# Twenty weight folds as ten units of 32x32-tile products, turned by VectorE

## The chip, the cores and the metric

The kernel runs on one NeuronCore of a Trainium2 chip. Its engines are named as the profile names them: PE is TensorE (PEld its weight loads), DVE is VectorE, ACT is ScalarE, POOL is GpSimd, and SP is SyncE, whose queue issues nearly all DMAs here. SBUF is the on-chip memory that all engines read; PSUM is the memory that TensorE writes and that VectorE and ScalarE read; this kernel keeps buffers (banks) of 128x512 numbers there, eight of them in the stage of the change. The metric is device time of one execution in microseconds (us), lower is better. Before the change three runs took 2378.09, 2379.88 and 2381.68 us; the median is 2379.88 us.

## What is computed

A sequence of 2048 rows of width 1024 is normalized; then a linear attention with 32 heads of width 32 runs beside a gated MLP, and their product is added to the input. In short:

```python
xn = layernorm(x)
q, k, v = heads(xn @ wqkv)                 # 32 heads of 32
pq, pk = q @ w_phi[h], k @ w_phi[h]        # one 32x32 matrix per head
phi = lambda p: concat(softmax(p), softmax(-p))
o = phi(pq) @ (phi(pk).T @ v) / (phi(pq) @ sum(phi(pk)))
s = o @ wo
g = silu((silu(xn @ w1) * (xn @ w3)) @ w2)
out = x + s * g
```

The step that the change touches is `pq = q @ w_phi[h]` and `pk = k @ w_phi[h]`. The kernel never forms q and k. It folds each head's 32x32 matrix into the 32 columns of that head in the weights, once, on the chip: `wk' = wk @ w_phi[h]`, `wq' = wq @ w_phi[h]`, for two weights of 1024x1024. After that, one product of xn with the folded weight gives pk or pq.

## The kernel before

All large products use fp32r operands that are split in a high and a low part, so that each product takes three passes. They are also done block by block in a scheme of seven products in place of eight (Strassen's kind); the seven are named by their left operands, in the order A11, A12, S2, S1, S3, S4, A22. Stages, by time in the profile: the gate and up products with w1 and w3 (to about 1130 us), the key, value and query heads (to about 1520), the down product with w2 (to about 2160), and the attention output with wo (to the end).

The change is in the first stage. It runs twice over 28 sections of the hidden width (`f`, once for each half of the rows, `tb`); a section is seven steps, one for each product, and `events` lists the steps in order. A step is 12 matmuls of 128x512 into a PSUM bank. A11, S2, S3 and A22 add up in a bank of kind b (two buffers), S1 and S4 in one of kind c (two buffers), and A12 alone uses bank a, which has one buffer. Partial sums are read while the section runs: ScalarE copies bank b after A11 (L625), VectorE adds bank a to that copy after A12 (L627) and adds bank b after S3 (L641), and so on. The next product into the same bank waits for that reader.

Beside the products, side work goes on, which each step carries in two lists, `before` (ahead of the step's matmuls) and `after` (behind them): loads of the next weights (`rw`), their sums and splits into operands `bo` (ScalarE casts the high part at L92, VectorE subtracts at L93), the preparation of the other half of the rows (`side_x`), of the key and value weights (`side_kv`, tiles `wkv`, `wkvo`), stores of the operands (`side_store`), and the folds. The order of all engines, SP's queue too, is written out by hand in this way; `room(step, cost)` moves a piece of VectorE work on to the first step in which VectorE's planned time stays under 2.55 us.

A fold (`fold`, L247) takes a piece of the transposed weight `wr` (128 columns of the weight on the partitions, four groups of 128 of them), and multiplies each of the four by a 128x128 block-diagonal matrix `bd` that holds four heads' `w_phi`. Only a quarter of `bd` is not zero. The product with `wr` as the stationary operand turns it as well, so that the result in PSUM (`pw`) has the weight's rows on the partitions; ScalarE copies it back to SBUF (L500) and SP stores it to DRAM. There are 32 folds. The first 12 run in the first 50 us, and `side_fold` spreads the other 20 over the steps from 67 on, one every 5 or 6 steps, each with its load 5 steps ahead and its store 2 steps behind. Four of the 20 belong to the key weight, and `side_kv` reads them back from DRAM; 16 are the query weight, which is read much later.

Of the kernel before, what the change touches and what calls it, by code (L numbers as in the profile page):

```python
# [8 lines left out]
F = mybir.dt.float32  # L9
# [8 lines left out]
P = 128  # L18
NT = S // P
ND = D // P  # L20
NF = FF // P
G = 8
# [7 lines left out]
def tile_kernel(ctx: ExitStack, tc: tile.TileContext, x, wkT, wqT, wv, wphi, wo, w1, w3, w2, out):  # L30
# [44 lines left out]
    wkv_d = [{n: dram.tile([P, 2, 4, 512], F, name=f"wkv_d{c}{n}") for n in BNAMES} for c in range(3)]  # L75
    wk_d = [[dram.tile([P, 512], F, name=f"wk_d{c}_{k}") for k in range(ND)] for c in range(2)]
    wq_d = [[dram.tile([P, 512], F, name=f"wq_d{c}_{k}") for k in range(ND)] for c in range(2)]

# [159 lines left out]
    def load_w(wT, dch, c, t=None):  # L238
        wr = blk("wr") if t is None else t
        nc.sync.dma_start(wr, wT[dch][:, 4 * c:4 * c + 4])  # L240
        return wr

    def fold(wr, c):

        pw = ps.tile([P, 4, P], F, name="pw", tag="tr", bufs=3)
        for g in range(4):
            nc.tensor.matmul(pw[:, g, :], wr[:, g], bd[:, 4 * c + g, :], start=True, stop=True)  # L247
        return pw

    folds = [(wkT, k, c, wk_d[c][k]) for c in range(2) for k in range(ND)]  # L250
    folds += [(wqT, k, c, wq_d[c][k]) for c in range(2) for k in range(ND)]

# [36 lines left out]

    phi_raw = flat(blk("phi")[:, :2]).rearrange("p (g f) -> p g f", f=DH)  # L290
    nc.sync.dma_start(phi_raw, wphi)
# [87 lines left out]
    def at(step, f, d=after):  # L379
        d.setdefault(step, []).append(f)  # L380
# [99 lines left out]
    def side_kv(c, k, s0):  # L480
# [8 lines left out]
        for n in BNAMES:  # L489
# [3 lines left out]
            at_ = store_quad(at_ + 1, wkv_d[1 + c][n][:, :, k], lambda src=src: (r + t2)[src], "wkvo", then)  # L493

    def side_fold(m, s0):
        wT, k, c, d = folds[m]
        w = []
        at(s0, lambda: w.append(load_w(wT, k, c)))
        at(s0 + 5, lambda: w.append(flat(fold(w[0], c))), before)
        at(s0 + 5, lambda: nc.scalar.copy(flat(w[0]), w[1]))  # L500
        at(s0 + 7, lambda: nc.sync.dma_start(d, flat(w[0])))

# [32 lines left out]
    for i in range(4, 8):  # L535
        side_x(i, FIRST_STEP + 13 * (i - 4))
    for m in range(FOLDS, len(folds)):
        side_fold(m, FIRST_STEP + 48 + 11 * (m - FOLDS) // 2)
    for m in range(8):
# [905 lines left out]
```

## Time and profile before

| what | value |
|---|---|
| median of three runs | 2379.88 us |
| the profiled execution, its own time | 2381.62 us |
| its span | 2379.8 us |
| TensorE busy | 2351.0 us (99%) |
| VectorE busy | 1760.9 us (74%) |
| ScalarE busy | 910.1 us (38%) |
| mean granted TensorE clock | 0.999 |

The page of the profile counts as busy time what an engine spends in instructions. The timeline merges neighbouring instructions of one line: start, busy time, engine, line, operation, tiles, shape and count. The start of a row minus the start of the row before it is what the earlier one took of TensorE's time, since its matmuls overlap at their ends. The view of the waits says who waited for whom. A matmul of type fp32 (as in the folds) is two matmul instructions in the trace, one of type fp32r is one.

### The profile page before, as it was taken

The page shows a single profiled execution, that of the slowest core. Times are in us where ns is not written, and L with a number is a line of the kernel's source. Part 1 is how long each engine was busy: PE and PEld are TensorE (multiplying, and loading weights), DVE is VectorE, ACT ScalarE, POOL GpSimd, SP SyncE. Part 2 cuts the span into 40 slices and gives each one's busy share as a digit, 9 for nine tenths or more (in the row PEclk, how much of TensorE's full clock was granted, in tenths as well). Part 3 has the DMA queues.
Part 4 walks back from the last instruction along what each step waited for, and adds up shares of the span by engine and source line. Part 5 has one row for each costly group of instructions (what it writes and reads, how often), then busy time and mean ns, then how long its engine had stood idle before and what let it go on. Part 6 is the DMA issues. An engine that isn't in the chain of part 4 may idle for free.

```text
span 2379.8 us, 37194 instructions
## 1 busy us (share of the span) xinstructions
PE 2351.0 (99%) x14348; PEld 1934.9 (81%) x14348; DVE 1760.9 (74%) x2729; ACT 910.1 (38%) x1597; POOL 257.6 (11%) x243
## 2 busy tenths in 40 slices
PE   7999999999999999999999999999999999999999
PEld 6788888888888888888788888887888888887887
DVE  8877788765688888875566666777678888786775
ACT  6445454543444554543212222334433333352000
POOL 1000000000000000000000000331012222213562
PEclk9999999999999999999999999999999999999999
DMA  5446699985998888865977878986435653478763
GB/s 215 146 155 212 230 354 332 328 266 186 289 303 283 292 306 289 268 209 195 384 287 277 306 253 307 364 315 249 159 124 151 204 177 133 156 245 272 213 179 103
DMA packets 291472, 578.00 MB, mean 243 GB/s; under 512 B 24912, under 2 KB 140768, under 8 KB 288608
## 3 DMA queue, kind: packets, MB, share of 16 engines
q1 hardware_dynamic: 284960, 552.56, 68.5%
q10 hardware_dynamic: 6336, 23.07, 2.5%
q8 instruction: 113, 1.85, 0.3%
q14 instruction: 63, 0.52, 0.1%
HBM read 372.64 MB, written 202.91 MB: 242 GB/s over the span
## 4 chain that ended last, share of the span: by engine, by line
PE 93%; DVE 3%; DMA 2%; ACT 1%; SPq 1%; issue 0%; POOL 0%; DVEq 0%; ACTq 0%; POOLq 0%
PE bankb L598 24%; PE bankb L1199 13%; PE bankc L598 12%; PE pm L1351 8%; PE bankb L794 7%; PE bankc L1199 6%; PE banka L598 6%; PE bankc L794 3%; PE banka L1199 3%; PE bankb L861 3%; PE banka L794 2%; PE bankc L861 1%; PE po L1336 1%; PE pkv L779 1%; PE pw L247 1%; PE banka L861 1%
## 5 line engine op out<-in xcount | busy, mean ns | idle before, releaser
L93 DVE TENSOR_TENSOR bo<-rw,bo 128x512 fp32r<-128x512 f32 x336 | 230.9, 689 | 158.2 <-ACT bo L92 155.4
L1199 PE MATMUL bankb<-bo,as 128*128 128x512 f32 x960 | 235.2, 389 | 1.2 <-ACT acc L1205 1.2
L1199 PEld LDWEIGHTS bankb<-bo,as 128*128 128x128 f32 x960 | 180.2, 188 | 39.0 <-ACT acc L1205 1.6
L92 ACT CAST bo<-rw 128x512 fp32r<-128x512 f32 x336 | 206.5, 617 | 13.8 <-DMA w_d2B<-w2o 3.4
L598 PE MATMUL bankb<-op0S,bo 128*128 128x512 f32 x672 | 164.6, 394 | 1.9 <-ACT op0S L92 1.2
L598 PE MATMUL bankc<-op0S,bo 128*128 128x512 f32 x672 | 162.2, 391 | 0.0
L1351 PE MATMUL pm<-wos,oT 128*128 128x512 f32 x672 | 161.1, 394 | 0.9 <-DVE oT L1342 0.9
L598 PE MATMUL bankb<-op1S,bo 128*128 128x512 f32 x672 | 161.4, 389 | 0.6 <-ACT u L633 0.6
L598 PE MATMUL bankc<-op1S,bo 128*128 128x512 f32 x672 | 161.2, 389 | 0.0
L598 PE MATMUL bankb<-op0A,bo 128*128 128x512 f32 x672 | 159.7, 391 | 0.8 <-DVE bo L93 0.5
L771 POOL MEMSET ev<- 128x32 f32 x32 | 4.1, 129 | 1427.1 <-DMA xoA<-xo_d0A 1073.2
L1199 PE MATMUL bankc<-bo,as 128*128 128x512 f32 x624 | 158.4, 389 | 0.0
L598 PE MATMUL bankb<-op1A,bo 128*128 128x512 f32 x672 | 157.6, 390 | 0.0
L598 PEld LDWEIGHTS bankb<-op0S,bo 128*128 128x128 f32 x672 | 126.3, 190 | 29.0 <-ACT op0S L92 1.6
L1351 PEld LDWEIGHTS pm<-wos,oT 128*128 128x128 f32 x672 | 124.7, 188 | 29.5 <-DVE oT L1342 1.7
L598 PEld LDWEIGHTS bankb<-op1A,bo 128*128 128x128 f32 x672 | 125.9, 188 | 27.4 <-DVE u L641 1.3
L598 PEld LDWEIGHTS bankb<-op1S,bo 128*128 128x128 f32 x672 | 126.1, 188 | 27.1 <-ACT u L633 1.0
L598 PEld LDWEIGHTS bankc<-op1S,bo 128*128 128x128 f32 x672 | 126.1, 188 | 26.2
L598 PEld LDWEIGHTS bankb<-op0A,bo 128*128 128x128 f32 x672 | 125.2, 188 | 26.9 <-DVE bo L93 0.8
L598 PEld LDWEIGHTS bankc<-op0S,bo 128*128 128x128 f32 x672 | 125.4, 188 | 25.6
L1199 PEld LDWEIGHTS bankc<-bo,as 128*128 128x128 f32 x624 | 117.2, 188 | 24.4
L1213 DVE TENSOR_TENSOR acc<-bankb,acc 128x512 f32<-128x512 f32 x152 | 102.0, 685 | 31.1 <-PE bankb L1199 31.1
(262 smaller groups left out, 4343.8 us busy)
## 6 DMA issues: line engine op xcount, KB each, us to landing
rw<-in_w SPq DMA_DIRECT2D x112, 512.0 KB, 4.4
hr<-h_d SPq DMA_DIRECT2D x56, 512.0 KB, 4.8
h_d<-h SPq DMA_DIRECT2D x111, 256.0 KB, 5.4
xoS<-xo_d0S SPq DMA_DIRECT2D x44, 512.0 KB, 6.2
xoS<-xo_d1S SPq DMA_DIRECT2D x44, 512.0 KB, 6.1
xoA<-xo_d0A SPq DMA_DIRECT2D x33, 512.0 KB, 4.9
xoA<-xo_d1A SPq DMA_DIRECT2D x33, 512.0 KB, 4.4
e_d<-eq ACTq DMA_DIRECT2D x32, 512.0 KB, 6.3
```

The lines of the kernel that those rows point to most:

```text
L92: nc.scalar.copy(hi, src)
L93: (by or nc.vector).tensor_sub(lo, src, hi.bitcast(F))
L247: nc.tensor.matmul(pw[:, g, :], wr[:, g], bd[:, 4 * c + g, :], start=True, stop=True)
L598: nc.tensor.matmul(bank[b], bos[tb, f][bn][:, w, k], ao[an][:, u, k], start=first and n == 0, stop=LAST[b] == an and n == 11, skip_group_c ...
L771: nc.gpsimd.memset(v[:, :, DH:], 1.0)
L779: nc.tensor.matmul(pkv[sl, m], e[:, m // 4, (m % 4) * P + 32 * h:(m % 4) * P + 32 * h + 32], v[:, 4 * (m % 4) + h], start=first and m == 0 ...
L794: nc.tensor.matmul(bank[b], xo[an][:, u, k], wb[bn][:, w, k], start=an in ("A11", "A12", "S1") and n == 0, stop=LAST[b] == an and n == 11, ...
L861: nc.tensor.matmul(bank[b], xo[an][:, u, k], wb[bn][:, w, k], start=an in ("A11", "A12", "S1") and n == 0, stop=LAST[b] == an and n == 11, ...
L1199: nc.tensor.matmul(bank[b], t[:, u, pos + k], bos[kb, bn, k][:, w], start=first and n == 0, stop=LAST[b] == an and n == 5, skip_group_chec ...
L1213: nc.vector.tensor_add(c, pb, c)
L1336: nc.tensor.matmul(po[32 * j:32 * j + 32, a, 64 * k:64 * k + 64], kvs[sl, j, c, k], et[sl, :, 4 * k + j], start=True, stop=True, skip_grou ...
L1351: nc.tensor.matmul(p, oTs[t, h][:, a, k], wos[c, 4 * h + k][:, b], start=n == 0, stop=n == 3 * ND - 1)
```

## The change

The 20 folds from step 67 on are replaced by ten units of another shape, at the steps 59, 68, 79, 89, 100, 110, 121, 131, 142 and 152. The first two units make the last four pieces of the key weight, the other eight the query weight.

- Operands. A unit now loads the transposed weight as it is into the room of `bd` (units 0 and 1: two pieces of 128x512, in runs of 128 numbers; units 2 to 9: one of 128x1024, a whole row of DRAM for each partition). `bd` is free by then, since only the first 12 folds need it. The matrices `w_phi` stay in `early_z`, which keeps them for the whole stage.
- Products. Instead of 128x128 by 128x128, a unit makes products of 32x32 by 32 x (32 nd): for each row strip j of the array (one of four heads) and each column strip q, `w_phi` of that head is stationary and a strided quarter of the weight moves. A unit has 16 products of 256 columns (units 2 to 9) or 32 of 128 columns (units 0 and 1). Each row strip writes a bank of its own: three of them are the banks of tag `tr`, which the transposes of x use too (named `pf`), and the fourth is bank a.
- Turning. The result is still transposed inside each 32x32 block. VectorE turns it with `transpose` from PSUM into the same room in SBUF: four instructions of 128x256 a unit, or eight of 128x128, in two pairs of places that `room` chooses at 0.7 us each. ScalarE's copies of `pw` are gone.
- DMA. A unit stores its result with one DMA in runs of 128 or 256 numbers. The next unit loads into the same room, so its load waits until that store has landed.

`room` now finds VectorE's time taken by the turns, and so it moves the pieces of `side_kv` some steps further on (its first piece ends at step 101 instead of 95, its last at 171 instead of 163).

```diff
@@ tile_kernel
-    wk_d = [[dram.tile([P, 512], F, name=f"wk_d{c}_{k}") for k in range(ND)] for c in range(2)]
-    wq_d = [[dram.tile([P, 512], F, name=f"wq_d{c}_{k}") for k in range(ND)] for c in range(2)]
+    wk_d = [[dram.tile([P, 512], F, name=f"wk_d{c}_{k}") for k in range(ND if c == 0 else 4)] for c in range(2)]
+    wk_late = dram.tile([4, P, 512], F, name="wk_late")
+    wk_d[1] += [wk_late[k] for k in range(4)]
+    wq_all = [dram.tile([ND, P, 512], F, name=f"wq_d{c}") for c in range(2)]
+    wq_d = [[wq_all[c][k] for k in range(ND)] for c in range(2)]
...
-    phi_raw = flat(blk("phi")[:, :2]).rearrange("p (g f) -> p g f", f=DH)
+    phi_raw = early_z.rearrange("p (g f) -> p g f", f=DH)
...
+    fold_free = [0]
+
     def side_fold(m, s0):
-        wT, k, c, d = folds[m]
-        w = []
-        at(s0, lambda: w.append(load_w(wT, k, c)))
-        at(s0 + 5, lambda: w.append(flat(fold(w[0], c))), before)
-        at(s0 + 5, lambda: nc.scalar.copy(flat(w[0]), w[1]))
-        at(s0 + 7, lambda: nc.sync.dma_start(d, flat(w[0])))
+        assert 1 < events[s0][2] < 6
+        w, banks = [flat(bd)], []
+        if m < 2:
+            gs_, nd = (4 + 2 * m, 5 + 2 * m), 4
+        else:
+            gs_, nd = (m - 2,), ND
...
+        def multiply():
+            banks.extend(ps.tile([P, 512], F, name="pf", tag="tr", bufs=3) for _ in range(3))
+            banks.append(ps.tile([P, 512], F, name="banka", bufs=BANKS["a"]))
+            for n, g in enumerate(gs_):
+                wn = w[0][:, 512 * n:512 * n + P * nd].rearrange("p (d k) -> p d k", d=nd)
+                for q in range(4):
+                    for j in (3, 0, 1, 2):
+                        sl = slice(32 * j, 32 * j + 32)
+                        nc.tensor.matmul(banks[j][32 * q:32 * q + 32, P * n:P * n + 32 * nd], phi_raw[sl, g], wn[sl, :, 32 * q:32 * q + 32],
+                                         start=True, stop=True, skip_group_check=True)
+
+        def turn(j):
+            for n in range(len(gs_)):
+                o = w[0].rearrange("p (d n f) -> p d n f", d=nd, f=DH)[:, :, 4 * n + j]
+                nc.vector.transpose(o, banks[j][:, P * n:P * n + 32 * nd].rearrange("p (d f) -> p d f", f=DH))
...
+        ready = max(s0 - 5, fold_free[0])
+        at(ready, load)
+        at(s0, multiply, before)
+        at_ = s0 - 1
+        for js in ((3, 0), (1, 2)):
+            at_ = room(at_ + 1, 0.7)
+            for j in js:
+                at(at_, lambda j=j: turn(j))
+        at(at_ + 2, store)
+        fold_free[0] = at_ + 4
...
-    for m in range(FOLDS, len(folds)):
-        side_fold(m, FIRST_STEP + 48 + 11 * (m - FOLDS) // 2)
+    for m, s0 in enumerate((59, 68, 79, 89, 100, 110, 121, 131, 142, 152)):
+        side_fold(m, s0)
```

The step of a unit decides between which two products it stands. Units 2, 4, 6 and 8 stand ahead of S2, straight behind A12; units 1, 3, 5, 7 and 9 stand ahead of S4; unit 0 stands ahead of S1. The rows that follow are from section 17 (the 18th), where unit 6 is. On TensorE, before: the two products, and the next fold one step on.

```order
L598 MATMUL bankb_3542<-op0A11_279,bo_3449 128x512 x12
L598 MATMUL banka_3565<-op0A12_280,bo_3477 128x512 [waits Activation_49]
L598 MATMUL banka_3565<-op0A12_280,bo_3477 128x512 x11
L598 MATMUL bankb_3542<-op0S2_281,bo_3500 128x512 [waits Activation_49]
L598 MATMUL bankb_3542<-op0S2_281,bo_3500 128x512 [waits DVE_49]
L598 MATMUL bankb_3542<-op0S2_281,bo_3500 128x512 x10
L247 MATMUL pw_3615<-bd_276,wr_3503 128x128 [waits DMAHW2_49,PE_49]
L247 MATMUL pw_3615<-bd_276,wr_3503 128x128 x3
```

Now unit 6 comes between A12 and S2, and its first small product goes into a new buffer of bank a, for which it waits for a DMA (the load of `bd`) and for DVE.

```order
L647 MATMUL bankb_3594<-op0A11_262,bo_3510 128x512 x12
L647 MATMUL banka_3617<-op0A12_263,bo_3533 128x512 [waits Activation_49]
L647 MATMUL banka_3617<-op0A12_263,bo_3533 128x512 x11
L524 MATMUL banka_3645<-bd_259,early_z_258 32x256 [waits DMAHW2_49,DVE_49]
L524 MATMUL pf_3642<-bd_259,early_z_258 32x256 [waits PE_49]
L524 MATMUL pf_3643<-bd_259,early_z_258 32x256 [waits PE_49]
L524 MATMUL pf_3644<-bd_259,early_z_258 32x256 [waits PE_49]
```

What moved: twelve more small products follow these four (the second to fourth column strip), and S2's matmuls behind them. Bank a's buffer before `banka_3645` is `banka_3617`, which VectorE reads when it adds A12's sum. On VectorE, before, the work around that sum (L627) was this.

```order
L93 TENSOR_TENSOR bo_3578<-rw_3252,bo_3578 128x512 [waits DMAHW0_49,Activation_49]
L128 TENSOR_TENSOR rw_3433<-rw_3433 128x512 [waits DMAHW6_49]
L129 TENSOR_TENSOR t2_3581<-rw_3433 128x512 [waits DMAHW5_49,DVE_49]
L93 TENSOR_TENSOR wkvo_3584<-wkv_3320,wkvo_3584 128x512 [waits PE_49,Activation_49]
L627 TENSOR_TENSOR h0_3563<-banka_3565,h0_3563 128x512 [waits DMAHW2_49,PE_49]
L93 TENSOR_TENSOR bo_3602<-rw_3252,bo_3602 128x512 [waits DMAHW1_49,Activation_49]
L93 TENSOR_TENSOR wkvo_3605<-wkv_3321,wkvo_3605 128x512 [waits Activation_49]
L93 TENSOR_TENSOR bo_3633<-rw_3433,bo_3633 128x512 [waits PE_49,Activation_49]
```

And this is VectorE's row of work at the same place now.

```order
L96 TENSOR_TENSOR bo_3630<-rw_3309,bo_3630 128x512 [waits DMAHW3_49,Activation_49]
L131 TENSOR_TENSOR rw_3494<-rw_3494 128x512 [waits DMAHW0_49]
L132 TENSOR_TENSOR t2_3633<-rw_3494 128x512 [waits DMAHW7_49,DVE_49]
L96 TENSOR_TENSOR wkvo_3636<-wkv_3357,wkvo_3636 128x512 [waits PE_49,Activation_49]
L676 TENSOR_TENSOR h0_3615<-banka_3617,h0_3615 128x512 [waits DMAHW4_49,PE_49]
L96 TENSOR_TENSOR bo_3674<-rw_3309,bo_3674 128x512 [waits Activation_49]
L530 STREAM_TRANSPOSE bd_259<-banka_3645 128x8x32 [waits DMAHW2_49,PE_49]
L530 STREAM_TRANSPOSE bd_259<-pf_3642 128x8x32
L96 TENSOR_TENSOR wkvo_3679<-wkv_3355,wkvo_3679 128x512 [waits DMAHW0_49,Activation_49]
L96 TENSOR_TENSOR bo_3702<-rw_3494,bo_3702 128x512 [waits Activation_49]
```

What moved: the four pieces of work ahead of the sum of bank a (L676 now, L627 before) are of the same kinds as they were; behind it stand the turns, which are new.

More of the change, by code (lines that the diff above doesn't have):

```diff
@@ L248, in fold @@
         return pw
-    folds = [(wkT, k, c, wk_d[c][k]) for c in range(2) for k in range(ND)]
-    folds += [(wqT, k, c, wq_d[c][k]) for c in range(2) for k in range(ND)]
+    folds = [(wkT, k, c, wk_d[c][k]) for c in range(2) for k in range(ND)][:FOLDS]
     def b_load(f):
@@ L1424 @@
         "wkT": lay(wqkv[:, D:2 * D]),
-        "wqT": lay(wqkv[:, :D]),
+        "wqT": wqkv[:, :D].T.reshape(G, P, D),
         "wv": wqkv[:, 2 * D:],
```

15 lines of the change are left out of this document (added).

## Prediction

> **What bounds the kernel now.** I read the page first (busy shares, then the chain that ended last), then the windows of the stage in which the 20 folds stand, then the timeline around one fold.
>
> ```profile
> span 2379.8 us, 37194 instructions
> PE 2351.0 (99%) x14348; PEld 1934.9 (81%) x14348; DVE 1760.9 (74%) x2729; ACT 910.1 (38%) x1597; POOL 257.6 (11%) x243
> PE 93%; DVE 3%; DMA 2%; ACT 1%; SPq 1%; issue 0%; POOL 0%; DVEq 0%; ACTq 0%; POOLq 0%
> 220.00:500.00 280.00, 280.00 (x1317) 234.33 (x1316) 218.97 (x347) 139.57 (x257) 0.00 (x0) 1.00 0.91 307
> ```
>
> The chain is TensorE's for 93%, and in the folds' stage (fourth line, columns: window, length, PE, PEld, DVE, ACT, POOL, clock, DMA share, GB/s) TensorE is busy 280 of 280 us at the full clock. There, what is taken from or given to TensorE's own row of work changes the time one for one; VectorE is idle for 61 us, ScalarE for 140.
>
> **What goes.** One fold on TensorE, and ScalarE's copies:
>
> ```profile
> 292.19 2.88 PE L598 MATMUL bankb<-op0S,bo 128*128 128x512 f32 x12
> 294.92 1.05 PE L247 MATMUL pw<-bd,wr 128*128 128x128 f32 x8
> 295.73 2.98 PE L598 MATMUL bankc<-op0S,bo 128*128 128x512 f32 x12
> 298.54 0.84 PE L598 MATMUL bankb<-op0A,bo 128*128 128x512 f32 x3
> L500 ACT COPY wr<-pw 128x512 f32<-128x512 f32 x18 | 10.6, 587 | 9.5 <-PE pw L247 9.5
> ```
>
> A product of twelve takes 294.92-292.19 = 2.73 us. The fold takes 295.73-294.92 = 0.81, and the product behind it 2.81, 0.08 more than its due: 0.90 us a fold. Twenty folds: -18.0 us, all on the path. The copies (20 of 0.59 us) were on ScalarE, which has room: 0.
>
> **What comes on TensorE.** No row shows 16 tiles of 32x32 at once. The nearest are the attention's products in 64x32 tiles (eight of them), and one fp32 product of 256 columns on the whole array:
>
> ```profile
> 2203.09 0.39 PE L1351 MATMUL pm<-wos,oT 128*128 128x512 f32 x1
> 2203.41 0.86 PE L1336 MATMUL po<-acc,kvs 64*32 64x64 f32 x64
> 2204.20 0.50 PE L1351 MATMUL pm<-wos,oT 128*128 128x512 f32 x1
> 2043.18 0.59 PE L1123 MATMUL us<-early_z,consts 128*128 128x256 f32 x2
> 2043.42 0.82 PE L1199 MATMUL bankb<-bo,as 128*128 128x512 f32 x2
> L1123 PE MATMUL us<-early_z,consts x2: 377/377/377, 2043.2 to 2043.4; 128*128 128x256 f32 x2
> ```
>
> The two instructions of the fp32 product of 256 columns start 0.59-0.377 = 0.21 us apart, so 64 columns stream in 0.053. The 64 instructions of the attention would need 3.4 us one after another and took 0.79: the eight tiles do run side by side (3.4/8 = 0.43) and the rest is the tail of the last one. A unit of 256 columns is 32 instructions on 16 tiles, two to a tile: 2x0.21 = 0.43 of streaming, some 0.2 until the last tile has started and 0.16 of tail, 0.79 by this estimate. Units 0 and 1 (64 instructions of 128 columns) stream for the same 0.43. As before and behind the attention's products some 0.2 us go to the change of shape (0.32 from the start of the last `pm` to the first `po` instead of 0.23, and a slower first product behind, as with the fold), I take 0.98 for each unit: +9.8 us. Lower end 0.59 a unit (the whole-array product, start to end); upper end 3.85 (second rival). If only eight tiles stream at a time, the row that is nearest, 0.43 more: +4.3 in all.
>
> [...]
>
> **The wait that comes with it.** Units 2, 4, 6 and 8 stand straight behind A12, and their first product writes bank a. So TensorE must wait until VectorE has added A12's sum, in four sections. In section 17:
>
> ```profile
> 384.68 2.88 PE L598 MATMUL banka<-op0A,bo 128*128 128x512 f32 x12
> 387.39 0.84 PE L598 MATMUL bankb<-op0S,bo 128*128 128x512 f32 x3
> 386.01 0.69 DVE L93 TENSOR_TENSOR bo<-rw,bo 128x512 fp32r<-128x512 f32 x1 [1.33 <-ACT bo L92]
> 386.62 0.69 DVE L128 TENSOR_TENSOR rw<-rw 128x512 f32<-128x512 f32 x1
> 387.34 0.69 DVE L129 TENSOR_TENSOR t<-rw 128x512 f32<-128x512 f32 x1
> 387.95 0.69 DVE L93 TENSOR_TENSOR wkvo<-wkv,wkvo 128x512 fp32r<-128x512 f32 x1
> 388.55 0.68 DVE L627 TENSOR_TENSOR h<-banka,h 128x512 f32<-128x512 f32 x1
> ```
>
> S2 starts at 387.39; the sum of bank a ends at 389.23, 1.84 later. Today nobody on TensorE waits for it. The new order has the same four kinds of work ahead of the sum in all four sections (a `wkvo` or `xo` split among them), and no fold between A11 and A12. From VectorE's end to TensorE's start another row tells the hop, in a wait of just this sort:
>
> ```profile
> 1149.92 2.23 PE L794 MATMUL bankc<-op2B,xoS 128*128 128x512 f32 x9
> 1153.03 0.76 PE L779 MATMUL pkv<-ev 128*32 128x34 f32 x64 [0.88 <-DVE ev L819]
> 1152.19 0.69 DVE L819 TENSOR_TENSOR ev<-bankc,ev 128x512 f32<-128x512 f32 x1 [1.96 <-PE bankc L794]
> 261.26 1.05 PE L247 MATMUL pw<-bd,wr 128*128 128x128 f32 x8
> 265.14 0.68 DVE L627 TENSOR_TENSOR h<-banka,h 128x512 f32<-128x512 f32 x1
> 264.89 2.88 PE L598 MATMUL bankb<-op0S,bo 128*128 128x512 f32 x12
> ```
>
> 1152.88 to 1153.03: 0.15. So a wait is 1.84+0.15-0.09 (the change of shape falls into it) = 1.9 us, four of them +7.6 us. All that TensorE has behind is held up with it; VectorE and ScalarE gain on TensorE by that. Lower end: in section 11 (last three lines) the sum ended only 0.93 behind S2's start, since a fold ahead of A12 had given VectorE time: 4x0.99 = 4.0.
>
> **VectorE's turns.** 32 of 128x256 and 16 of 128x128:
>
> ```profile
> L1179 DVE STREAM_TRANSPOSE acc<-acc 128x1024 f32<-128x1024 f32 x30 | 35.5, 1220 | 0.0
> L641 DVE TENSOR_TENSOR u<-bankb,u 128x512 f32<-128x512 f32 x14 | 9.6, 685 | 0.2 <-PE bankb L598 0.2
> ```
>
> 1220 ns for 1024 columns is at least 0.31 us for 256; an operation on 512 columns of PSUM takes 0.69. I take 0.37 and 0.22: 32x0.37+16x0.22 = 15.4 us, in the 61 idle ones. What may be late next is the sum after S3, for which A22 waits:
>
> ```profile
> 315.77 2.88 PE L598 MATMUL bankc<-op0S,bo 128*128 128x512 f32 x12
> 318.49 5.60 PE L598 MATMUL bankb<-op0A,bo 128*128 128x512 f32 x24
> 317.23 0.68 DVE L641 TENSOR_TENSOR u<-bankb,u 128x512 f32<-128x512 f32 x1
> ```
>
> Here it ended 0.58 us before A22 began, in a section that had a fold of 0.90 in between and eleven pieces of work on VectorE between the sums of bank a and b. Without the fold A22 would wait 0.90-0.58+0.15 = 0.47. In the new order eleven such pieces without a unit stand in sections 16, 19 and 22: 3x0.47 = +1.4 at most, +1.0 taken. The others have eight to ten, or a unit that gives VectorE time.
>
> **DMA.** Twenty loads and twenty stores become twelve and ten, of the same bytes, in runs of 512 B in the stores.
>
> ```profile
> rw<-in_w SPq DMA_DIRECT2D x16, 512.0 KB, 5.2
> xo_d0S<-op0S SPq DMA_DIRECT2D x15, 512.0 KB, 7.4
> SPq L256 <- DVE bo L93: 56.2, 14, 5.8
> ```
>
> The room is one, so a load waits on SP's queue for the store before it: 7.4 (a store in such runs) and 5.2 us, 12.6 from the last turn to the loaded room; the next unit comes at least 8 steps of 2.73 us behind the last turn, and 6 (16 us) behind the store's place in the queue. Queued behind the waiting load are the `rw` loads; those wait for VectorE 4 us each anyway (third line). I put it at 0, upper end 3 us.
>
> **Sum.** -18.0+9.8+7.6+1.0 = +0.4 us: 2381.62 (the profiled execution: 2379.8 of span and 1.8 around it) becomes 2382.0, and the median of runs, 1.74 lower, 2380.3. Within 0.2% (4.8 us), about what a measurement of this kernel can tell from no change.
>
> **Rivals.** First, faster: VectorE comes to bank a earlier (the 4.0 of section 11's row) and a unit costs 0.65, near the lower end: -18.0+6.5+4.0 = -7.5, 2372.4. For it: ScalarE, whose casts VectorE waits for, has 12 us less to do. Against: the 1.33 us in the row at 386.01 are ScalarE waiting for A11's bank, not for copies.
>
> Second, slower by the array: the two halves of an fp32 product follow each other in one tile, and if a product must wait in order behind them, a unit of 256 columns takes 16x0.21+0.4 = 3.85 us, one of 128 the same: +28.7 over my sum, 2409. [...] The attention's row speaks against it: 32 pairs at 0.053 would be 1.7 us, and it took 0.79.
>
> Third, slower by VectorE: with turns in its row, the sum after S3 comes late in all eleven sections that have no wait on bank a, by 0.47 and two turns' 0.3 us: 11x0.77-1.0 = +7.5, 2387.8. It decides from the point where eleven pieces or more stand between the two sums; for it the 0.58 above, against it the count of eight to ten in most sections.
>
> **How the numbers follow.** Forecast (within 0.2%) 0.50, with eight tiles at a time counted in (+4.3); first rival 0.19; second 0.06; third, with a load of the room that comes late, 0.25. So faster 0.19, same 0.50, slower 0.31. The forecast's own range is 2376 to 2385. For 8 in 10 it must reach down to most of the first rival (2373) and up past the third (2389); the second stays out.
>
> **What would show it.** Right: `pw` rows are left for 12 folds only; small products with an idle of about 1.7 us before them, put down to VectorE's sum of bank a, four times; about 1.0 us from the first small product to the next large one; turns of 0.3 to 0.4 us. Wrong: an idle before the small products put down to a DMA; waits of A22 for VectorE in most sections; or a unit of several us.

## The result, and the profile after

| | kernel before | changed kernel |
|---|---|---|
| median of 17 runs each | 2379.63 us (2378.09 to 2382.71) | 2385.06 us (2379.74 to 2390.81) |
| ratio, 95% interval | | 1.0021 (1.0014 to 1.0029) |
| profiled execution, its own time / span | 2381.62 / 2379.8 us | 2383.72 / 2381.9 us |
| TensorE busy | 2351.0 us | 2344.6 us |
| A12 of section 8 to A12 of section 26 (all units stand between) | 364.71 us | 366.75 us |

The change costs 5.4 us on the median, 0.2%. The forecast was 2380.3; the time lies in its range (2373 to 2389) and outside the forecast's own range by a hair (2376 to 2385). The runs of the changed kernel also lie wider apart, over 11 us instead of under 5; why is not shown.

The page's second line, and what TensorE waited for longest in the changed kernel (us in total, times, longest):

```profile
PE 2344.6 (98%) x14572; PEld 1920.8 (81%) x14572; DVE 1772.7 (74%) x2777; ACT 900.1 (38%) x1577; POOL 256.7 (11%) x243
PE pw L250 <- DMA room_b<-in_wkT: 7.4, 1, 7.4
PE banka L524 <- DVE h L676: 6.9, 4, 1.7
PE pt L221 <- DVE xt L216: 3.2, 1, 3.2
PE pm L1400 <- ACT acc L1102: 3.0, 1, 3.0
```

The first and third wait stand at the start and were there before (7.3 and 3.7). The second and fourth are new. The second is the forecast one: four waits of 1.7 us for VectorE's sum of bank a. The fourth, at the first product with `wo` some 1700 us later, stands nowhere in the prediction.

The stretch of the folds, answering the row shown of before (window, length, PE, PEld, DVE, ACT, POOL, clock, DMA share, GB/s), and two short windows in it:

```profile
220.00:500.00 280.00, 273.05 (x1484) 220.34 (x1483) 220.12 (x370) 126.33 (x231) 0.00 (x0) 0.99 0.87 287
328.90:332.30 3.40, 3.40 (x9) 2.67 (x8) 1.91 (x4) 0.44 (x1) 0.00 (x0) 0.50 1.08 392
451.80:455.20 3.40, 3.40 (x9) 2.66 (x10) 1.96 (x4) 0.81 (x2) 0.00 (x0) 0.50 1.14 314
```

TensorE is idle for 7 us of the 280, all of it the four waits, and for two stretches of 3.4 us its granted clock is 0.50 (half clock, in what follows). Each begins about a microsecond behind one of the waits. A profile is one execution, and half clock stands elsewhere too: in the profiled execution of before the clock is 0.50 from 62.1 to 65.5 us, in that of the changed kernel it is 1.00 there (first row before, second row changed):

```profile
62.10:65.50 3.40, 3.40 (x9) 2.62 (x10) 3.40 (x7) 1.10 (x3) 0.00 (x0) 0.50 0.32 133
62.10:65.50 3.40, 3.40 (x16) 2.81 (x15) 3.40 (x6) 1.53 (x3) 0.00 (x0) 1.00 0.17 70
```

The changed kernel comes to A12 of section 8 1.4 us earlier (199.01 instead of 200.40); a stretch of half clock costs 1.6 us, as shown below. So the two spans, 2.1 us apart, must not be set against the medians' 5.4 part for part. The first of the four waits (section 11), from the timelines of TensorE and VectorE:

```profile
261.84 0.69 DVE L96 TENSOR_TENSOR bo<-rw,bo 128x512 fp32r<-128x512 f32 x1 [1.33 <-ACT bo L95]
264.38 0.68 DVE L676 TENSOR_TENSOR h<-banka,h 128x512 f32<-128x512 f32 x1
265.12 0.40 PE L524 MATMUL banka<-bd,early_z 32*32 32x256 f32 x1 [1.74 <-DVE h L676]
265.46 0.39 PE L524 MATMUL pf<-bd,early_z 32*32 32x256 f32 x3
265.77 0.50 PE L647 MATMUL bankb<-op0S,bo 128*128 128x512 f32 x1
```

The sum ends at 265.06 and the first small product starts 0.06 later. From there to S2's first product it is 0.65 us; the last small ones start 0.34 after the first. A unit without a wait, and a unit of the other shape (64 instructions of 128 columns):

```profile
292.29 2.88 PE L647 MATMUL bankb<-op0S,bo 128*128 128x512 f32 x12
295.11 0.40 PE L524 MATMUL banka<-bd,early_z 32*32 32x256 f32 x1
295.75 3.01 PE L647 MATMUL bankc<-op0S,bo 128*128 128x512 f32 x12
298.60 1.75 PE L647 MATMUL bankb<-op0A,bo 128*128 128x512 f32 x7
204.54 0.29 PE L524 MATMUL banka<-bd,early_z 32*32 32x128 f32 x1
205.54 1.20 PE L647 MATMUL bankc<-op0S,bo 128*128 128x512 f32 x4
```

S3 is due to end at 292.29+2.72 = 295.01; the next product (S4) starts at 295.75 and takes 2.85 to its successor instead of 2.72: 0.87 us for the unit. The other shape takes 1.00 from its first small product to the next large one, and with what it loses ahead and behind 1.22: section 8 takes 21.59 instead of 20.37 before, where it has the same transpositions of x and no fold.

The half clock behind the wait in section 14, and the turns on VectorE (from the view of the tile `pf`: duration min/median/max in ns):

```profile
327.70 0.40 PE L524 MATMUL banka<-bd,early_z 32*32 32x256 f32 x1 [1.74 <-DVE h L676]
328.36 4.60 PE L647 MATMUL bankb<-op0S,bo 128*128 128x512 f32 x12
332.79 2.88 PE L647 MATMUL bankc<-op0S,bo 128*128 128x512 f32 x12
L530 DVE STREAM_TRANSPOSE bd<-pf x36: 272/406/444, 208.7 to 486.7; 128x256 f32<-128x256 f32 x24, 128x128 f32<-128x128 f32 x12
```

S2 takes 332.79-328.36 = 4.43 us; behind a unit at full clock a product takes 2.85. Whole sections say the same: section 14 takes 23.31 us here and 21.75 in a kernel below that has the same wait and no half clock, so one such stretch costs 1.6 us. And the wait at the first product with `wo`, of before and then of the changed kernel (timeline of TensorE):

```profile
2164.82 1.71 PE L1336 MATMUL po<-acc,kvs 64*32 64x64 f32 x128
2166.47 5.22 PE L1351 MATMUL pm<-wos,oT 128*128 128x512 f32 x21
```

```profile
2165.34 1.71 PE L1385 MATMUL po<-acc,kvs 64*32 64x64 f32 x128
2170.03 4.96 PE L1400 MATMUL pm<-wos,oT 128*128 128x512 f32 x21 [2.98 <-ACT acc L1102]
```

Nothing in this part of the program was changed.

### The profile page after: what moved, and what is told of

Read it like the earlier page. It is cut to its first block, busy times and chain, and to the rows that moved or that the text cites. A ratio compares the mean times of both kernels' runs of the same rounds, so it can differ in the third digit from the quotient of the medians.

```text
span 2381.9 us, 37605 instructions
## 1 busy us (share of the span) xinstructions
PE 2344.6 (98%) x14572; PEld 1920.8 (81%) x14572; DVE 1772.7 (74%) x2777; ACT 900.1 (38%) x1577; POOL 256.7 (11%) x243
## 4 chain that ended last, share of the span: by engine, by line
PE 91%; DVE 3%; DMA 3%; ACT 1%; SPq 1%; issue 1%; POOL 0%; DVEq 0%; ACTq 0%; POOLq 0%
PE bankb L647 24%; PE bankb L1248 13%; PE bankc L647 12%; PE pm L1400 8%; PE bankb L843 7%; PE bankc L1248 6%; PE banka L647 5%; PE bankc L843 3%; PE banka L1248 3%; PE bankb L910 3%; PE banka L843 2%; PE bankc L910 1%; PE po L1385 1%; PE pkv L828 1%; PE banka L910 1%; DMA op2T<-wkv_d1T 1%
```

## The experiments

Each kernel is compared with the kernel before, run beside it on the same chip. The stretch from A12 of section 8 to A12 of section 26, which holds all ten units or, in before, all 20 folds, serves as a second measure of time; its length is free of what the rest of the program does. Half clock and waits are those of the one profiled execution of each kernel. "Code shifted by 64" means that 64 instructions whose results nobody uses stand ahead of TensorE's work; why follows below.

| kernel | median us | ratio to before (95%) | section 8 to 26, us | waits for bank a | half clock in it | wait at first `wo` product, us |
|---|---|---|---|---|---|---|
| before | 2379.63 | | 364.71 | 0 | 0 | 0 |
| changed | 2385.06 | 1.0021 (1.0014 to 1.0029) | 366.75 | 4 | 2 | 3.0 |
| units 2, 4, 6, 8 one step later | 2381.29 | 1.0006 (0.9997 to 1.0015) | 362.79 | 0 | 1 (6.8 us) | 2.8 |
| before, four folds into bank a | 2387.99 | 1.0030 (1.0019 to 1.0041) | 372.19 | 4 | 0 | 0 |
| changed, no turns | 2385.04 | 1.0020 (1.0011 to 1.0029) | 363.63 | 4 | 0 | 3.4 |
| six units behind A12 | 2398.25 | 1.0075 (1.0061 to 1.0089) | 369.21 | 6 | 1 | 3.2 |
| no unit behind A12 | 2392.06 | 1.0047 (1.0035 to 1.0060) | 355.96 | 0 | 0 | 4.1 |
| the same, code shifted by 64 | 2388.69 | 1.0031 (1.0018 to 1.0043) | 355.96 | 0 | 0 | 0 |
| before, code shifted by 192 | 2385.03 | 1.0020 (1.0011 to 1.0029) | 364.71 | 0 | 0 | 3.1 |
| before, code shifted by 64 | 2381.56 | 1.0007 (0.9998 to 1.0016) | 364.71 | 0 | 0 | 0 |
| changed, code shifted by 64 | 2378.98 | 0.9993 (0.9984 to 1.0002) | 366.76 | 4 | 2 | 0 |
| the same, waits filled by 16 products | 2385.58 | 1.0021 (1.0011 to 1.0030) | 370.62 | 0 | 0 | 0 |
| the same, filled by 8 | 2381.99 | 1.0007 (0.9997 to 1.0016) | 363.57 | 0 | 0 | 0 (2.4 elsewhere) |
| changed, one unit behind A12, code shifted by 64 | 2374.00 | 0.9972 (0.9960 to 0.9983) | 358.45 | 1 | 0 | 0 |

The theory at first was the prediction's: four waits for bank a, to which the trace had added half clock behind them. Its rivals were that the waits only take up time another wait would take, and that VectorE's turns are what costs.

### Four units one step later

```
-    for m, s0 in enumerate((59, 68, 79, 89, 100, 110, 121, 131, 142, 152)):
+    for m, s0 in enumerate((59, 68, 80, 89, 101, 110, 122, 131, 143, 152)):
```

> Units 2, 4, 6 and 8 stand one step later (80, 101, 122, 143), ahead of S1 instead of S2, so that VectorE has read bank a long before. Theory of the wait (the four waits for VectorE's sum of bank a, 1.9 us each in the trace of the change, and the stretches of 3.4 us at half the clock that follow two of them, 1.6 us each, are the loss; units themselves cost some 9 us for the 18 that the folds took): 7 to 10 us faster than before, about 2371, no wait of TensorE in the stage, granted clock as in the kernel before, and runs as close together as those of before. Theory of VectorE (its 48 turns and the side work that they push on are the loss, and a wait of TensorE only shows it): the wait turns up at another product, and the time stays 0 to 6 us above before. Theory of the transfers (stores in short runs, one room, and the 3.0 us wait at the first wo product): 0 to 5 us above before.

```profile
PE pt L221 <- DVE bd L530: 3.4, 1, 3.4
PE pm L1400 <- ACT acc L1102: 2.8, 1, 2.8
```

All four waits are gone, but unit 2, now at step 80, holds the three transposition banks when the transpositions of x at the next steps want them: one wait of 3.4 us, with 6.8 us of half clock at it. In the stretch there is a gain (4.0 us shorter than in the changed kernel), and the wait at the first `wo` product stays. The 7 to 10 us under before that were expected on the median did not come: 1.0006 is no difference that can be told from none.

### The waits alone

In the kernel before, the folds at steps 79, 100, 121 and 142 write bank a instead of a transposition bank (three of them are moved to that place by 1 or 2 steps):

```
+        if in_a:
+            pw = ps.tile([P, 512], F, name="banka", bufs=BANKS["a"]).rearrange("p (g n) -> p g n", g=4)
```

> The kernel before, with its 20 large folds; only four of them are put into bank a straight behind A12, at steps 79, 100, 121 and 142, as units 2, 4, 6 and 8 are in the change. Theory of the wait: four waits of about 2.0 us, +8 us, and up to four stretches at half the clock of up to 1.7 us each: 8 to 13 us slower than before, with a wider spread of runs. Theories of VectorE and of the transfers: none of their causes is here, so within 1 us of before.

```profile
PE banka L250 <- DVE h L631: 6.3, 4, 1.7
```

7.4 us more than before, a little under the 8 to 13 expected; in the stretch 372.19-364.71 = 7.5. The four waits alone cost 1.9 us each, with no unit and no turn in the program, and none is followed by half clock. The wait at the `wo` product is not there.

### No turns

```
-            for j in js:
-                at(at_, lambda j=j: turn(j))
```

> The change without VectorE's 48 turns (left out; the folded weights of the last ten units are then not what the reference has, and all the rest runs on them; the places of all other work are unchanged). Theory of the wait: within 2 us of the change, the four waits still there at 1.7 us of idle. Theory of VectorE: 4 us or more faster than the change, at or below the kernel before. Theory of the transfers: as the change.

```profile
PE banka L524 <- DVE h L674: 6.9, 4, 1.7
PE pm L1398 <- ACT acc L1100: 3.4, 1, 3.4
```

The time is that of the changed kernel, and both new waits are as they were: the 48 turns cost nothing. The stretch is 3.1 us shorter than in the changed kernel, and all of it lies in the two sections that had half clock there (14 and 20: 21.75 and 21.77 here, 23.31 and 23.34 there); the other sections agree to 0.06 us. So the difference is the clock's and not the turns'.

### Six units behind A12

```
+    for m, s0 in enumerate((58, 72, 81, 93, 102, 114, 123, 135, 144, 156)):
```

> The change with its ten units at the steps 58, 72, 81, 93, 102, 114, 123, 135, 144 and 156: six of them straight behind A12 instead of four. Theory of the wait: six waits of 1.9 us, that is 3.8 us more than the change, and 0 to 3 us more at half the clock: 8 to 13 us slower than before. Theories of VectorE and of the transfers: the same work, so as the change, 3 to 7 us slower than before.

```profile
PE banka L524 <- DVE h L676: 9.8, 6, 1.7
PE bankb L647 <- ACT u L682: 8.5, 2, 8.1
```

Six waits, as planned; with them 13 us more than the changed kernel. But the 8.1 us are a new wait near 578 us that has nothing to do with bank a (it comes back in the next kernel), so of this run only the stretch counts: 369.21, of it 1.6 for one half clock, so 367.6 against 363.6 with four waits and none. Section by section, against the kernel below that has no unit behind A12, the six waits cost 1.6 to 1.9 us each, 10.7 together; 0.9 more goes to section 11, where a unit at step 81 stands near transpositions of x (one wait of 0.7).

### No unit behind A12

```
+    for m, s0 in enumerate((59, 67, 87, 96, 108, 116, 124, 136, 144, 152)):
```

> The ten units stand behind the products of S2, S1 or S3 at steps 59, 67, 87, 96, 108, 116, 124, 136, 144 and 152, none behind A12 and none beside a transposition of x. Theory (each wait of TensorE for VectorE's sum of bank a costs its 1.74 us, and two of the four are followed by 3.4 us at half clock that cost 1.7 us more): no wait for bank a by the products of the units, no stretch of half clock between 200 and 500 us, and the first stage some 10 us shorter than in the changed kernel; the 3 us wait of TensorE ahead of the first product with wo stays, so about 2374 us, 0.25% under the kernel before. Rival (the units themselves cost about what the folds did): within 2 us of the changed kernel's 2385.

In the stretch the theory holds: 355.96, which is 363.63-355.96 = 7.67 us under the kernel with four waits and no half clock, and 8.75 under the kernel before. Of the 7.67, 0.28 is a wait of A22 in section 19; the sections with the four waits are 1.83 to 1.86 us longer each, 7.4 together. But the time is 12 us over before. Two lines of TensorE's waits, two of SP's between 515 and 592 us, and one of ScalarE's timeline:

```profile
PE bankb L647 <- ACT u L682: 13.3, 1, 13.3
PE pm L1400 <- issue: 4.1, 1, 4.1
```

```profile
SPq L167 <- DVE wkvo L96: 24.3, 1, 24.3
SPq L167 <- PE bankb L647: 12.4, 1, 12.4
575.72 0.63 ACT L680 ACTIVATE h<-h 128x512 f32<-128x512 f32 x1 [16.37 <-DVE h L676]
```

With other steps for the units, `room` puts the last pieces of `side_kv` later, and the loads of the next half's `op1A` on SP's queue wait 24.3 us for VectorE's splits in them. The stores of `h` stand behind those loads in the queue, so the tiles that VectorE and ScalarE need come free late, and TensorE waits 13.3 us for ScalarE. Half clock stands at that wait too (566.2 to 583.3 us), and section 26 takes 35.34 us instead of 19.04, 16.3 more. The six-waits kernel has the same wait at the same place. This chain is read from the order of the queue and the waits; no run takes it apart, so it is argued and not shown.

### Where TensorE's code is cut

The wait ahead of the first product with `wo` remained. The profile names ScalarE for it in the changed kernel, "issue" (nothing that the profile shows) in the kernel with no unit behind A12, and a DMA in one run below; it is there in all kernels with the ten units and not in the two that have folds. Two theories: the change has 18 DMAs fewer, which moves the order of the semaphores that DMAs share; or it is TensorE's own code. The queue "q8 instruction" of before and of the changed kernel (packets, MB):

```profile
q8 instruction: 113, 1.85, 0.3%
q8 instruction: 115, 1.88, 0.3%
```

1.85 MB in 113 packets are 16.4 KB each. TensorE has 14,348 products, as many weight loads and 330 waits and the like in before, 29,026 instructions in all, and 29,026/113 = 257 to a packet; in the changed kernel 29,473/115 = 256. In both traces packet n of this queue (from 0) starts when TensorE has begun between 256n+150 and 256n+449 of its instructions, for every n. So these packets are read here as TensorE's code, 256 instructions each. Counted in the trace in order of start, from 0, the first product with `wo` is instruction 23,553 in before, 1 behind a multiple of 256, and 24,000 in the changed kernel, 192 behind one (the units have 224 products and 224 weight loads more than the folds, 448 = 256+192, and there is one wait fewer). In the changed kernel TensorE stops just before number 24,001. A packet of the queue starts in that pause, at 2167.78, and has landed at 2168.66; TensorE goes on 1.4 us after that. In all seven kernels that stop like this the last packet landed 1.3 to 1.6 us before TensorE went on. The instructions ahead are the attention's 128 products and 128 weight loads, 256 instructions in 1.71 us.

To shift the code, n small products of the identity matrix, which nobody reads, go ahead of TensorE's first work, in its idle time (each is four instructions; with the waits that come with them the count at the first `wo` product moves by 66 for 16 of them and by 193 for 48):

```
+    pad = [ps.tile([P, 512], F, name="pad", tag="tr", bufs=3) for _ in range(3)]
+    for m in range(16):      # 48 in the kernel shifted by 192
+        nc.tensor.matmul(pad[m % 3][:32, :32], ident[:32, :32], ident[:32, :32], start=True, stop=True)
```

The kernel with no unit behind A12, shifted by 64:

> The kernel with the units behind S2, S1 and S3, and ahead of TensorE's first work 16 small products of 32x32 (64 instructions of TensorE) whose results nobody reads. The trace loads TensorE's code in blocks of 256 instructions, and in the changed kernel the first product with wo stands at the border of two blocks, right behind 256 instructions that take 1.7 us. Theory (TensorE waits there for its code): the border lies elsewhere, the 3 us wait ahead of the first product with wo is gone, and the time is 1.3 to 3 us under that of the same kernel without the 16 products, about 2371 us. Rival (the wait is for a transfer of wo, whose place in the order of transfers has moved): the wait of 3 us stays, and the time is the same.

The kernel before, shifted by 192, which puts its first `wo` product where the changed kernel has it:

> The kernel before with 48 small products of 32x32 (192 instructions of TensorE) ahead of TensorE's first work, in its idle time, whose results nobody reads: the border of two code blocks then lies at the first product with wo, as in the changed kernel, and nothing else of the change is made. Theory (code): TensorE waits some 3 us ahead of the first product with wo, and the time is 1.3 to 3 us over the kernel before, about 2382 us, less what an earlier start at full clock may give, up to 1.7 us. Rival (order of transfers): no wait there, and the kernel before's time.

The changed kernel, shifted by 64 (448+64 = 512, so its code is cut, to one instruction, where that of before is):

> The changed kernel with the 16 small products ahead of TensorE's first work. Theory (code): the four waits for bank a stay as they are, 6.9 us in all, the 3 us wait ahead of the first product with wo is gone, and the time is 1.3 to 3 us under the changed kernel's, about 2383 us. Rival (order of transfers): wait and time as in the changed kernel, 2385 us.

TensorE's timeline, of the kernel before shifted by 192 and of the changed kernel shifted by 64:

```profile
2162.38 1.71 PE L1339 MATMUL po<-acc,kvs 64*32 64x64 f32 x128
2167.15 2.19 PE L1354 MATMUL pm<-wos,oT 128*128 128x512 f32 x5 [3.06 <-DMA wos<-wo_d]
```

```profile
2164.86 1.71 PE L1388 MATMUL po<-acc,kvs 64*32 64x64 f32 x128
2166.50 5.26 PE L1403 MATMUL pm<-wos,oT 128*128 128x512 f32 x21
```

The wait comes into a kernel that has nothing of the change, and goes out of the changed one with all of its 22 DMAs in their order. The theory of the code holds, the one of the order of the DMAs falls. In time: +5.0 us on the kernel before (1.0020), -6.1 on the changed kernel's median (2378.98 against 2385.06, run at different times, each against before on its own chip: 0.9993 against 1.0021), -3.4 on the kernel without units behind A12 (of 5 and 6 runs, with intervals that overlap, so this figure alone would not show it). The first two are more than the 3 us of the wait, and more than the 1.3 to 3 expected. In the trace of the shifted kernel before, 3.4 us of half clock follow the wait (2167.5 to 2170.9), worth some 1.6 by the sections above; half clock is there too in five of the other six kernels with such a wait, and in the changed kernel's one profiled execution it is not. 3.1+1.6 = 4.7 is near the 5.0, but that profiled execution took 2382.56, 2.5 under its kernel's median, so the likeness proves little: the wait is shown, and what the medians lose beyond it is in part open.

A counter-test, the kernel before with 16 of the small products:

> The kernel before with 16 small products (64 instructions) ahead of TensorE's first work instead of 48: the same kind of added work, but the border of the code blocks lies some 128 instructions behind the first product with wo. Theory (the place of the border alone decides): no wait ahead of the first product with wo, and the kernel before's time within 2 us. Rival (the added products themselves cost time, or any shift does): slower by a third of the 5.0 us that 48 products cost, or more.

1.0007 (0.9998 to 1.0016), no wait: neither the small products themselves nor a shift as such is what costs.

### The waits filled, and where half clock follows

In the changed kernel shifted by 64, TensorE multiplies identity matrices into one of the unit's own banks while it would wait for bank a:

```
+            if m in (2, 4, 6, 8):
+                for _ in range(16):      # 8 in the second kernel
+                    nc.tensor.matmul(banks[0][:, :P], ident, ident, start=True, stop=True, skip_group_check=True)
```

> The changed kernel with the 16 small products ahead of TensorE's first work, and ahead of the products of units 2, 4, 6 and 8 sixteen products of the 128x128 identity with itself, into one of the unit's own banks, which the unit's products then overwrite: TensorE works through the 1.74 us in which it waited for bank a, and the border of the code blocks stays where it is. Theory (a wait of 1.74 us beside a unit's small products is what takes the clock to half): no stretch of half clock between 200 and 500 us, and 1.7 us less for each stretch that there was, two in the profiled execution without the filling: about 2376 us against 2379. Rival (the clock falls by the unit's small products, or at random): stretches of half clock stay, and the time is 2379 to 2381.

> As the kernel with the filled waits, but with eight identity products ahead of each of the four units instead of sixteen, which took 3.7 us there, twice the wait of 1.74 us: eight take some 1.85 us, so TensorE works through the wait and hardly longer (0.1 us for each unit). The border of the code blocks moves by 128 instructions and lies some 60 instructions behind the first product with wo, in work that takes longer than the load. Theory (the wait beside the small products takes the clock to half): no stretch of half clock between 200 and 500 us, section lengths as with the waits but without the sections of 23.3 us, and 1 to 3 us less than the 2379.0 of the same kernel without filling. Rival (half clock comes by the small products, or costs nothing on the median): 2379 to 2380.

Sixteen took 3.7 us, not the 1.87 that they were meant to take (each is two matmul instructions), so the stretch is 7.0 us longer than with four bare waits (4x1.8), and the kernel says only that no half clock came in it. With eight the work fits the wait (1.9 us), and the stretch is 363.57, as long as with four bare waits and no half clock (363.63), 3.2 under the kernel it is made from, which had two half clocks. Eight filled waits in these two kernels, none followed by half clock; the bare ones, of units or of folds, were followed by it in 5 of 23 in the six profiled executions that have them. By these counts alone, eight in a row without it would come by chance once in seven.

The times in the traces say more. In their clock records each stretch of half clock that ends within the span is 3.413 us long or a whole multiple of it, and in each execution the stretches begin whole multiples of 3.413 us apart (in before at 14.31 and 62.10 us: 14 multiples; in the changed kernel at 14.85, 328.88 and 451.76 us: 92 and 36). Counted on from these starts, an execution divides into intervals of 3.413 us, and every wait has a place in one. The changed kernel's four began 0.50, 0.89, 1.32 and 2.77 us into an interval, and half clock followed the first two of these. Of all 19 bare waits ahead of units:

| the wait began, us behind the start of an interval | waits | half clock in the next interval |
|---|---|---|
| 0.07 to 0.91 | 5 | 5 |
| 0.98 to 3.07 | 14 | 0 |

A wait of about 1.15 us near 60 us, which all 14 kernels have (with one of 0.6 close behind it), shows the same: the five that began 0.15 to 0.75 us into an interval were followed by half clock, as in before (0.75), and the other nine, as in the changed kernel (3.17), were not. Units without a wait never were (72, of which 16 began in the first 0.91 us). So at these places half clock goes with the wait, when it falls early in an interval. Three limits stay. Only two of the eight filled waits began that early (0.67 and 0.76), so the filling itself is tested by two cases. Of the four waits ahead of folds one began at 0.45 and was not followed. And near 1158 us TensorE waits for `xoA` 1.09 us in before and 1.31 in the changed kernel, both from 0.51 us into an interval, and the clock stays at 1.00. Why is open.

The median did not follow: 2381.99, above the 2378.98 of the unfilled kernel, where 2376 to 2378 were expected. Its trace has two waits that the other has not, 1.9 us at 605 us for VectorE's operand `bo`, and this:

```profile
2177.58 0.81 PE L1391 MATMUL po<-acc,kvs 64*32 64x64 f32 x58
2180.79 0.31 PE L1391 MATMUL po<-acc,kvs 64*32 64x64 f32 x6 [2.40 <-issue]
```

The fillers move the code by another 128. At the first `wo` product that is harmless, but another border now falls into a later group of the attention's products, between the 58th and the 59th of 64 that wait for nobody; the instruction that comes late is number 24,513 = 24,001+512. By this reading the code is late at yet another place, and 3.4 us at half clock follow (2182.4 to 2185.8).

### One unit behind A12

```
+    for m, s0 in enumerate((59, 68, 79, 89, 101, 110, 122, 131, 143, 152)):
```

and the 16 small products ahead of TensorE's first work.

> The changed kernel with the 16 small products ahead of TensorE's first work, and units 4, 6 and 8 one step later, behind the products of S2 instead of A12; unit 2 keeps its place. Theory (waits for bank a): one wait of 1.7 us is left of four, and with three waits go 3 times 1.74 us and, as far as half clock followed them, 1.7 us each for up to two: 5 to 8.6 us under the 2379.0 of the same kernel with four waits, so 2370 to 2374 us, 0.3% or more under the kernel before. Rival (the waits only move time that another wait then takes): 2377 to 2379 us.

```profile
PE banka L527 <- DVE h L679: 1.7, 1, 1.7
220.00:500.00 280.00, 278.25 (x1521) 224.80 (x1520) 227.54 (x382) 129.16 (x238) 0.00 (x0) 1.00 0.90 296
```

2374.0 us, 0.9972 (0.9960 to 0.9983): under both kernels, at the upper end of the 2370 to 2374 expected. The stretch is 358.45, 2.5 over the kernel with no wait (1.8 for the wait, 0.7 for two waits of A22 of 0.3), and 8.3 under the changed kernel. The rival that the waits only take up time which another wait would take falls.

## Why the prediction was right or wrong

The time was inside the range, and the sum for the part that was summed was near: +0.4 forecast, -1.1 measured in the stretch without half clock. But +5.4 came in all, since a term was missing. That the range held is luck: its upper part stood for VectorE's turns coming late and for a late load of the room, and neither came.

- **Folds removed: -18.0.** Right. From A12 to A12 a section with one fold takes 19.95 us, one without 19.04: 0.91 each, 18.2.
- **Ten units at 0.98: +9.8.** Near, slightly over-sized. Eight of 0.87 and two of 1.22: +9.4. The case that the sum is built on (sixteen tiles at once) holds, and the eight-tiles case and the second rival fall: 32 instructions take 0.65 us in all. (That rival's 16x0.21+0.4 is 3.76, not 3.85, so its +28.7 would be +27.8.) The change of shape costs 0.13 behind a unit and 0.1 ahead of it. The sign "about 1.0 us from the first small product to the next large one" came for two units and was 0.65 for eight.
- **Four waits at 1.9: +7.6.** Right, in size and place: 7.4, 1.83 to 1.86 each, by the sections of two kernels whose units stand at other steps. The hop from VectorE's end to TensorE's start was 0.06 us instead of 0.15. The first rival's 1.0 a wait did not come; ScalarE was busy 10 us less (910.1 to 900.1) and VectorE came no earlier.
- **Half clock behind the waits.** Missing from the sum. The prediction took the clock as 1.00 throughout and did not ask what a wait of 1.7 us does to it. In the changed kernel's profiled execution it cost 366.75-363.63 = 3.1 us; it comes in some executions and not in others, for the waits ahead of units by where they fall in the intervals of 3.413 us.
- **A22 waiting for VectorE: +1.0.** Over-sized. One such wait of 0.3 us is left in the changed kernel (section 19 takes 19.38 instead of 19.04). The sections 16 and 22, which the prediction counted too, have none. The third rival did not come at all.
- **Turns hidden: 0.** Right, by the kernel without them, though each takes 0.41 to 0.44 us instead of the 0.37 estimated.
- **DMA: 0.** Right; no product of a unit waited for its load.
- **The step that failed** is the sum's silent one, that nothing outside the units' stage moves. The change gives TensorE 448 instructions more, and with them every later border between blocks of its code moves by 192 instructions, one of them onto the first product with `wo`, behind the attention's burst. TensorE then stands still 3.0 us there. That cost 5.0 us on the median of a kernel with nothing else changed, and without it the changed kernel stands at 0.9993 of before (0.9984 to 1.0002).

By the terms as measured the units' stage without half clock comes to -18.2+9.4+7.4+0.3 = -1.1 us, and the stretch says 363.63-364.71 = -1.1. Two half clocks make it +2.0 in the profiled execution. On the medians the changed kernel is 5.4 over before, and with its code shifted 1.1 under it (2378.98 against 2380.07), though its profiled execution then still has two half clocks in the stretch. So by the medians the whole loss goes with the place of the border. Of these 6 us the traces show 3.0 us of standing still and, in six of the seven kernels that stop, half clock at it; the rest is open.

## What to carry to other kernels

When a change alters how many instructions an engine has, count them, and look where the borders of its code blocks go. Here a block, as read from the packets of the queue q8 (one to 256 or 257 of TensorE's instructions), is 256 instructions, and where such a border lay at the end of a burst that ran through 256 in 1.7 us, far from the place of the change, TensorE stood still 2.8 to 4.1 us. A wait whose named releaser changes from kernel to kernel, or that is put down to "issue", is a hint of it; a few instructions that do nothing, ahead of the program, test it in one run. And a unit of work that can go behind any of several products should not write the bank that the product just ahead of it leaves to another engine.

## What the runs showed of the hardware

- **Code arrives late, as the counts and the shifts are read.** Seven times, once in each of seven kernels, TensorE stood still at an instruction whose number is 193 modulo 256 in that count. It went on 4.6 to 5.7 us after it had passed the border before (6.9 in the kernel with the waits filled by eight, where the packet started 4.2 us behind that border instead of 2.2 to 3.2 and took 1.4 us instead of 0.9). Other blocks that took 4.2 us went through without a stop in the same kernels (in the changed kernel the one from number 24,769 on, 2201.76 to 2206.00 us). The block size is that of the packets of the queue q8, one to 257 of TensorE's instructions in before and to 256 in the changed kernel. Behind a block whose work takes some 1.7 us TensorE stood still 2.8 to 4.1 us in six kernels, and 2.4 in the seventh, behind a block of 4.3 us whose packet started late.
- **A wait of 1.74 us was followed by half clock or not, by where it fell.** Five of 23 waits for bank a were followed by 3.4 us at a granted clock of 0.50, each of which made its section 1.6 us longer: the five of units that began in the first 0.91 us of an interval of 3.413 us, and none of the 14 that began later in one. The intervals are those of the clock records, whose stretches of half clock begin whole multiples of 3.413 us apart (14 in before, 92 and 36 in the changed kernel). It is not so at every place: a wait ahead of a fold that began at 0.45, and two of 1.09 and 1.31 us near 1158 us that began at 0.51, were not followed.
- **Sixteen tiles of 32x32 do run at once in fp32.** 32 instructions of 256 columns took 0.65 us from the first to the next large product, 64 of 128 columns 1.00. In section 11 of the changed kernel the first 16 of the 32 start within 0.10 us (265.12 to 265.22), and each takes 0.40 or 0.41.
